# Loading the first 256 rows of x with two neighbouring rows per partition in a SwiGLU kernel

## The chip, the cores and the metric

The kernel runs on one core of a Trainium2 chip. The metric is the device time of one execution in microseconds (us), taken as the median of several runs; lower is better.

## The reference

The reference is a gated feed-forward layer, all tensors bf16:

```python
B, S, D, F = 1, 2048, 640, 1536     # x: (B, S, D)
g = silu(x @ w_gate)                # w_gate: (D, F)
u = x @ w_up                        # w_up:   (D, F)
return (g * u) @ w_down             # w_down: (F, D)
```

## The kernel before

The 2048 rows of x (tokens) are cut into four blocks of 512 (`S_BLK`), and each block into four chunks of 128. D = 640 is five slices of 128 (`KD`, index kd), F = 1536 is twelve (`KF`, index fc or kf).

**A block.** For each fc, `proj` (L197) multiplies the gate weights and the up weights with xT, the transposed x: five matmuls of 512 columns each into the PSUM tiles pg and pu (four buffers in all). `gate` (L212) applies Silu on ScalarE (pg to sg) and multiplies by pu on VectorE into aT. After twelve fc, the down projection follows. Output columns 512 to 639 of all the block's tokens come from twelve matmuls into po_t (L274); ScalarE copies that to ot_t (L283), VectorE transposes it in 32 x 32 squares into ot_q (L285), and ScalarE issues four stores of it (L287), one for each 32 columns, in pieces of 64 bytes. Output columns 0 to 511 come chunk by chunk: twelve matmuls into po_a (L303; the pool tag has two buffers), a copy to ot on ScalarE (L312), a store from SyncE's queue (SP, L321).

**The start.** Tokens 0 to 255 (`PE_X` = 2 chunks) come into x_sb as rows and are transposed on TensorE (`transpose_chunk`, L185: ten transposes into pt, copies to xT by ScalarE for kd 0 and 1 and by VectorE for kd 2 to 4). All other tokens are transposed by the DMA on the way in (`turn_x`, L108). While x is under way, TensorE runs 20 matmuls on ones (`warm`, L175). Then `head` (L221) runs the gate matmuls of fc 0 and 1 for the first 256 tokens: eight of 128 columns for kd 0 and 1 (first chunk 0, then chunk 1), six of 256 columns for kd 2 to 4. Ten up matmuls of 256 columns follow, and then tokens 256 to 511 of the same two fc.

**The first loads.** A DMA is started by the queue of an engine, in the order of that queue. SP starts x chunk 0, the gate weights of fc 0 and 1 for kd 0 and 1 (`K_CUT` = 2), the up weights for kd 2 to 4, and then the transposing load of tokens 256 to 511; ScalarE starts x chunk 1 and the gate weights for kd 2 to 4, and then loads its function table; GpSimd starts the up weights for kd 0 and 1. SP goes on with the rest of the weights, w_down (wd_sb), the next blocks of x and transposed copies of the weights (wgT, wuT).

**Other work.** The last four tokens are computed on VectorE (`row_dots`, L143: 96 multiply-and-sum instructions of x_row with wgT and wuT), spread between VectorE's other work.

**Order.** The head's order on TensorE, ScalarE and GpSimd, and the whole order on VectorE and SP, is kept as written (`keep_order`, L98). From the first block's loop on, the order on TensorE and ScalarE is decided when the program is built: a scheduler goes by its own estimate of when each instruction can run. DMAs started by SP and ScalarE take one of eight completion counters in turn, and a DMA whose counter is still in use waits for the earlier DMA on it.

Of the kernel before, what the change touches and what calls it, by code (L numbers as in the profile page):

```python
# [10 lines left out]
def _body(  # L11
# [8 lines left out]
    nc = tc.nc  # L20
    P = nc.NUM_PARTITIONS
# [8 lines left out]
    x2 = x.rearrange("b s d -> (b s) d")  # L30
    out2 = out.rearrange("b s d -> (b s) d")

    KD = D // P
    KF = F // P
    S_BLK = 512
    NSB = S // S_BLK
    SUB = S_BLK // P
    DA = 512
    Q = 32
# [3 lines left out]
    PE_X = 2  # L43
    K_CUT = 2
# [12 lines left out]
    x_sb = consts.tile([P, PE_X, D], bf16)  # L57
    xT = consts.tile([P, KD, S], bf16)
    wg_sb = consts.tile([P, KD, F], bf16)
    wu_sb = consts.tile([P, KD, F], bf16)  # L60
# [9 lines left out]

    make_identity(nc, ident[:])

    x_v = x2.rearrange("(c p) d -> p c d", p=P)
    xt_v = x2.rearrange("s (kd p) -> s kd p", p=P)
    wg_v = w_gate.rearrange("(kd p) f -> p kd f", p=P)
    wu_v = w_up.rearrange("(kd p) f -> p kd f", p=P)
    wd_v = w_down.rearrange("(kf p) d -> p kf d", p=P)

    def wslice(a, b):
        return slice(a * P, b * P)  # L80

    def load_w(eng, dst, src, a, b):
        eng.dma_start(out=dst[:, :, wslice(a, b)], in_=src[:, :, wslice(a, b)])

    def load_x(eng, c0, c1):
        eng.dma_start(out=x_sb[:, c0:c1, :], in_=x_v[:, c0:c1, :])

    def issue_order(a, b):
        tc.add_manual_dep(
# [18 lines left out]
    def turn_x(c0, c1):  # L108
        s_sl = slice(c0 * P, c1 * P)
        nc.sync.dma_start_transpose(out=xT[:, :, s_sl], in_=xt_v[s_sl])  # L110

    load_x(nc.sync, 0, 1)
    load_x(nc.scalar, 1, 2)
    f_sl = wslice(*W_CHUNKS[0])
    for dst, src, first, second in (
        (wg_sb, wg_v, nc.sync, nc.scalar),
        (wu_sb, wu_v, nc.gpsimd, nc.sync),
    ):
        for eng, k_sl in ((first, slice(0, K_CUT)), (second, slice(K_CUT, KD))):
            eng.dma_start(out=dst[:, k_sl, f_sl], in_=src[:, k_sl, f_sl])  # L120
    turn_x(PE_X, SUB)
    nc.scalar.activation(silu_first[:], ones[:, 0:1], ACT.Silu)
    for a, b in W_CHUNKS[1:]:
# [6 lines left out]
    def turn_w(dst, src):  # L130
# [7 lines left out]
        out=x_row[:],  # L138
        in_=x2[S - T : S, :].rearrange("t d -> (t d)").partition_broadcast(P),
# [29 lines left out]
    def do_dots(n):  # L169
        for _ in range(n):  # L170
            next(dots, None)
# [3 lines left out]
    def warm(n):  # L175
        for _ in range(n):
            nc.tensor.matmul(  # L177
                pw[:, 0:P],
                lhsT=ones[:].broadcast_to([P, P]),
                rhs=ones[:].broadcast_to([P, P]),  # L180
                start=True,
                stop=True,
            )

    def transpose_chunk(c, parts):  # L185
        c_sl = slice(c * P, (c + 1) * P)
        for copy, tag, k0, k1 in parts:
            pt = psum.tile([P, k1 - k0, P], bf16, tag=tag, name="pt")
            for kd in range(k0, k1):
                nc.tensor.transpose(  # L190
                    out=pt[:, kd - k0, :],
                    in_=x_sb[:, c, kd * P : (kd + 1) * P],
                    identity=ident[:],
                )
            copy(out=xT[:, k0:k1, c_sl], in_=pt[:])  # L195

    def proj(ps, w_sb, fc, sb, c0, c1):  # L197
        for kd in range(KD):
            nc.tensor.matmul(  # L199
                ps[:, c0:c1],  # L200
                lhsT=w_sb[:, kd, fc * P : (fc + 1) * P],
                rhs=xT[:, kd, sb * S_BLK + c0 : sb * S_BLK + c1],
                start=(kd == 0),
                stop=(kd == KD - 1),
            )

    def gu_tiles():
        pg = psum.tile([P, S_BLK], f32, tag="gu", name="pg", bufs=4)
        pu = psum.tile([P, S_BLK], f32, tag="gu", name="pu", bufs=4)
        return pg, pu  # L210

    def gate(pg, pu, sb, fc, n_s):  # L212

        s0 = sb * S_BLK
        sg = work.tile([P, S_BLK], f32, name="sg")
        nc.scalar.activation(sg[:, 0:n_s], pg[:, 0:n_s], ACT.Silu)  # L216
        nc.vector.tensor_tensor(  # L217
            out=aT[:, fc, s0 : s0 + n_s], in0=sg[:, 0:n_s], in1=pu[:, 0:n_s], op=ALU.mult
        )

    def head():  # L221

        dve, act = nc.vector.tensor_copy, nc.scalar.copy
        split = [(act, "po_a", 0, 2), (dve, "po_b", 2, KD)]
        late = PE_X * P
        (pg0, pu0), (pg1, pu1) = gu_tiles(), gu_tiles()  # L230
        warm(N_WARM)
        transpose_chunk(0, split)
        transpose_chunk(1, split)
        early = [(kd, c * P, (c + 1) * P) for c in range(PE_X) for kd in range(K_CUT)]
        early += [(kd, 0, late) for kd in range(K_CUT, KD)]
        for kd, c0, c1 in early:
            for fc, pg in ((0, pg0), (1, pg1)):


                nc.tensor.matmul(  # L240
                    pg[:, c0:c1],
                    lhsT=wg_sb[:, kd, wslice(fc, fc + 1)],
                    rhs=xT[:, kd, c0:c1],
                    start=(kd == 0 and c0 == 0),
                    stop=(kd == KD - 1),
                )
        proj(pu0, wu_sb, 0, 0, 0, late)
        proj(pu1, wu_sb, 1, 0, 0, late)
        for fc, pg, pu in ((0, pg0, pu0), (1, pg1, pu1)):
            proj(pg, wg_sb, fc, 0, late, S_BLK)  # L250
            proj(pu, wu_sb, fc, 0, late, S_BLK)
            gate(pg, pu, 0, fc, S_BLK)
        keep_order(mybir.EngineType.PE)
        keep_order(mybir.EngineType.Activation)
        keep_order(mybir.EngineType.Pool)

    head()
    for sb in range(NSB):
        n_s = S_BLK if sb < NSB - 1 else S_BLK - T
        for fc in range(KF):  # L260
            if sb == 0 and fc < 2:
                continue
            pg, pu = gu_tiles()
            proj(pg, wg_sb, fc, sb, 0, n_s)
            proj(pu, wu_sb, fc, sb, 0, n_s)
            gate(pg, pu, sb, fc, n_s)
            if sb > 0 and fc < KF - 2:
                do_dots(2)


        n_t = (SUB if sb < NSB - 1 else SUB - 1) * P
        po_t = psum.tile([P, n_t], f32, tag="po_b", name="po_t")
        for kf in range(KF):
            nc.tensor.matmul(  # L274
                po_t[:],
                lhsT=wd_sb[:, kf, DA:D],
                rhs=aT[:, kf, sb * S_BLK : sb * S_BLK + n_t],
                start=(kf == 0),
                stop=(kf == KF - 1),
            )  # L280
        ot_t = outp.tile([P, n_t], bf16, name="ot_t")
        ot_q = outp.tile([P, n_t], bf16, name="ot_q")
        nc.scalar.copy(ot_t[:], po_t[:])  # L283
        do_dots(3)
        nc.vector.transpose(out=ot_q[:], in_=ot_t[:])  # L285
        for q in range(P // Q):
            nc.scalar.dma_start(  # L287
                out=out2[
                    sb * S_BLK : sb * S_BLK + n_t, DA + q * Q : DA + (q + 1) * Q
                ].rearrange("(i r) c -> r i c", r=Q),  # L290
                in_=ot_q[q * Q : (q + 1) * Q, :].rearrange("r (i c) -> r i c", c=Q),
            )

        for j in range(SUB):
            s0 = sb * S_BLK + j * P
            last = sb == NSB - 1 and j == SUB - 1
            cols = [(0, DA, "po_a")]
            if last:
                cols = [(0, DA // 2, "po_a"), (DA // 2, DA, "po_a"), (DA, D, "po_b")]
            for c0, c1, tag in cols:  # L300
                po = psum.tile([P, c1 - c0], f32, tag=tag, name="po_a")
                for kf in range(KF):
                    nc.tensor.matmul(  # L303
                        po[:],
                        lhsT=aT[:, kf, s0 : s0 + P],
                        rhs=wd_sb[:, kf, c0:c1],
                        start=(kf == 0),
                        stop=(kf == KF - 1),
                    )
                ot = outp.tile([P, c1 - c0], bf16, name="ot" if c1 < D else "ot_b")  # L310
                if c1 < D:
                    nc.scalar.copy(ot[:], po[:])  # L312
                    eng = nc.sync
                else:
                    nc.vector.tensor_copy(out=ot[:], in_=po[:])  # L315
                    eng = nc.sync
                if 0 < j and not last:
                    do_dots(3)
                if sb == NSB - 1 and j == ROW_J:
                    row_tail()  # L320
                eng.dma_start(out=out2[s0 : s0 + P, c0:c1], in_=ot[:])  # L321
        if sb == 0:
            turn_x(2 * SUB, 3 * SUB)
            turn_w(wuT, wut_v)
            turn_x(3 * SUB, 4 * SUB)
# [107 lines left out]
```

## Time and profile before

| what | value |
|---|---|
| median of 3 runs | 163.68 us (163.44 to 163.95) |
| the profiled execution | 163.61 us, of which 162.2 us are the span of its instructions |
| TensorE matmul busy | 159.8 us, 98% of the span |
| VectorE busy | 110.8 us (68%) |
| ScalarE busy | 42.9 us (26%) |
| chain that ended last | TensorE 97%, DMA 2% |
| TensorE from 0 to 2.77 us | 20 warm-up matmuls; x_sb lands at 2.77 |
| TensorE after the last matmul to the end of the span | 1.9 us |

In rows of the profile, PE is TensorE, PEld its weight loads, DVE VectorE, ACT ScalarE, POOL GpSimd, SP SyncE; SPq, ACTq and POOLq are the queues that start DMAs. L190 is line 190 of the kernel. A group's row gives its busy time, the mean duration of one instruction in ns, and the idle time of its engine just before it. A row of the waits reads "who waited <- for whom: us in total, times, longest". A row of the chain or the timeline gives the start in us, the duration, and what ran; a bracket is idle time before it, and what ended that. A row of the DMA issues ends with the time from issue to landing.

### The profile page before, as it was taken

The numbers are of one execution on the slowest core, as the hardware profiler recorded it, in microseconds if no ns is written. First come the engines' busy times: TensorE is split into PE (matmuls) and PEld (weight loads), VectorE is DVE, ScalarE is ACT, GpSimd is POOL, SyncE is SP. The second block draws the span as 40 slices with busy tenths as digits, with TensorE's granted clock in tenths as the row PEclk, the third lists the DMA queues.
The fourth block names the chain that finished last, engine by engine and source line by source line (L and its number), as shares of the span: only waits on it lengthen the run. The fifth ranks groups of instructions, "written<-read, shape, count | busy, mean of one in ns | idle before, by whom it ended". The sixth has DMA issues, their size and how long they took to land.

```text
span 162.2 us, 2119 instructions
## 1 busy us (share of the span) xinstructions
PE 159.8 (98%) x798; PEld 78.1 (48%) x798; DVE 110.8 (68%) x249; ACT 42.9 (26%) x74; POOL 1.5 (1%) x7
## 2 busy tenths in 40 slices
PE   8999999999999999999999999999999999999995
PEld 8854444444444444444444444444444444445454
DVE  1042233599469999979919999979964999993000
ACT  5132222112222222221222322221214222222121
POOL 3000000000000000000000000000000000000000
PEclk9999999999999999999999999999999999999999
DMA  7999999993179996003110000000320000000212
GB/s 215 275 343 350 363 217 220 240 216 87 35 164 161 205 177 136 4 0 34 65 65 0 0 4 2 0 0 1 63 68 33 0 0 0 0 0 4 50 39 73
DMA packets 42217, 15.86 MB, mean 98 GB/s; under 512 B 33216, under 2 KB 42048, under 8 KB 42208
## 3 DMA queue, kind: packets, MB, share of 16 engines
q1 hardware_dynamic: 33680, 14.75, 37.6%
q10 hardware_dynamic: 8480, 0.85, 3.4%
q8 instruction: 6, 0.10, 0.3%
q0 software_dynamic: 48, 0.13, 0.2%
q14 instruction: 3, 0.02, 0.1%
HBM read 6.88 MB, written 2.62 MB: 59 GB/s over the span
## 4 chain that ended last, share of the span: by engine, by line
PE 97%; DMA 2%; DVE 0%; issue 0%
PE pu L199 32%; PE pg L199 31%; PE po_a L303 26%; PE po_t L274 6%; DMA x_sb<-in_x_dram 2%; PE pg L240 1%; PE pt L190 1%; DVE ot_b L315 0%
## 5 line engine op out<-in xcount | busy, mean ns | idle before, releaser
L199 PE MATMUL pu<-xT,wu_sb 128*128 128x512 bf16 (+2 forms) x250 | 59.7, 370 | 0.0
L199 PE MATMUL pg<-xT,wg_sb 128*128 128x512 bf16 (+2 forms) x240 | 58.5, 374 | 0.0
L217 DVE TENSOR_TENSOR aT<-sg,pu 128x512 bf16<-128x512 f32 (+1 forms) x48 | 32.8, 684 | 32.4 <-PE pu L199 28.1
L216 ACT ACTIVATE sg<-pg 128x512 f32<-128x512 f32 (+1 forms) x48 | 28.6, 597 | 70.8 <-PE pg L199 66.2
L303 PE MATMUL po_a<-wd_sb,aT 128*128 128x512 bf16 (+2 forms) x216 | 42.8, 358 | 0.0
L148 DVE SCALAR_TENSOR_TENSOR prod<-wgT,x_row 128x640 f32<-128x640 bf16 x48 | 39.4, 821 | 1.1
L148 DVE SCALAR_TENSOR_TENSOR prod<-wuT,x_row 128x640 f32<-128x640 bf16 x48 | 39.4, 822 | 1.0
L199 PEld LDWEIGHTS <-wu_sb 128*128 128x128 bf16 x250 | 24.5, 98 | 27.3
L199 PEld LDWEIGHTS <-wg_sb 128*128 128x128 bf16 x240 | 23.5, 98 | 26.9
L303 PEld LDWEIGHTS <-aT 128*128 128x128 bf16 x216 | 20.7, 98 | 21.6
L312 ACT CAST ot<-po_a 128x512 bf16<-128x512 f32 (+1 forms) x17 | 9.5, 561 | 32.0 <-PE po_a L303 20.9
L274 PE MATMUL po_t<-aT,wd_sb 128*128 128x512 bf16 (+1 forms) x48 | 10.4, 366 | 0.0
L274 PEld LDWEIGHTS <-wd_sb 128*128 128x128 bf16 x48 | 4.7, 98 | 5.1
L315 DVE CAST ot_b<-po_a 128x128 bf16<-128x128 f32 x1 | 0.3, 292 | 9.9 <-PE po_a L303 9.9
L283 ACT CAST ot_t<-po_t 128x512 bf16<-128x512 f32 (+1 forms) x4 | 2.2, 559 | 11.6 <-PE po_t L274 11.6
L148 DVE DVE_READ_ACCUMULATOR prod<-wuT,x_row 128x1 f32 x48 | 4.0, 83 | 0.0
L148 DVE DVE_READ_ACCUMULATOR prod<-wgT,x_row 128x1 f32 x48 | 3.9, 82 | 0.0
L285 DVE STREAM_TRANSPOSE ot_q<-ot_t 128x512 bf16<-128x512 bf16 (+1 forms) x4 | 2.7, 678 | 1.7 <-ACT ot_t L283 1.7
L195 DVE COPY xT<-pt 128x384 bf16<-128x384 bf16 x2 | 0.7, 358 | 3.5 <-PE pt L190 3.5
L177 PE MATMUL pw<-ones 128*128 128x128 bf16 x20 | 2.3, 310 | 0.3 <-DVE ones L106 0.3
L240 PE MATMUL pg<-xT,wg_sb 128*128 128x128 bf16 (+1 forms) x14 | 2.2, 347 | 0.0
L177 PEld LDWEIGHTS <-ones 128*128 128x128 bf16 x20 | 2.0, 144 | 0.3 <-DVE ones L106 0.3
(16 smaller groups left out, 8.4 us busy)
## 6 DMA issues: line engine op xcount, KB each, us to landing
wd_sb<-in_w_down_dram SPq DMA_DIRECT2D x1, 1920.0 KB, 14.0
out_dram<-ot SPq DMA_DIRECT2D x15, 128.0 KB, 1.7
wg_sb<-in_w_gate_dram SPq DMA_DIRECT2D x2, 640.0 KB, 8.2
wu_sb<-in_w_up_dram SPq DMA_DIRECT2D x2, 640.0 KB, 8.8
x_row<-in_x_dram SPq DMA_DIRECT2D x1, 640.0 KB, 5.2
out_dram<-ot_q ACTq DMA_DIRECT2D x12, 32.0 KB, 1.9
wg_sb<-in_w_gate_dram SPq DMA_DIRECT2D x1, 320.0 KB, 4.4
wu_sb<-in_w_up_dram SPq DMA_DIRECT2D x1, 320.0 KB, 4.9
```

What stands on the lines that cost most here:

```text
L148: nc.vector.scalar_tensor_tensor(out=prod[:], in0=wT[:, fc, :], scalar=1.0, in1=x_row[:, t, :], op0=ALU.mult, op1=ALU.mult, accum_out=acc[ ...
L177: nc.tensor.matmul(pw[:, 0:P], lhsT=ones[:].broadcast_to([P, P]), rhs=ones[:].broadcast_to([P, P]), start=True, stop=True,)
L190: nc.tensor.transpose(out=pt[:, kd - k0, :], in_=x_sb[:, c, kd * P : (kd + 1) * P], identity=ident[:],)
L199: nc.tensor.matmul(ps[:, c0:c1], lhsT=w_sb[:, kd, fc * P : (fc + 1) * P], rhs=xT[:, kd, sb * S_BLK + c0 : sb * S_BLK + c1], start=(kd == 0 ...
L216: nc.scalar.activation(sg[:, 0:n_s], pg[:, 0:n_s], ACT.Silu)
L217: nc.vector.tensor_tensor(out=aT[:, fc, s0 : s0 + n_s], in0=sg[:, 0:n_s], in1=pu[:, 0:n_s], op=ALU.mult)
L240: nc.tensor.matmul(pg[:, c0:c1], lhsT=wg_sb[:, kd, wslice(fc, fc + 1)], rhs=xT[:, kd, c0:c1], start=(kd == 0 and c0 == 0), stop=(kd == KD ...
L274: nc.tensor.matmul(po_t[:], lhsT=wd_sb[:, kf, DA:D], rhs=aT[:, kf, sb * S_BLK : sb * S_BLK + n_t], start=(kf == 0), stop=(kf == KF - 1),)
L283: nc.scalar.copy(ot_t[:], po_t[:])
L285: nc.vector.transpose(out=ot_q[:], in_=ot_t[:])
L303: nc.tensor.matmul(po[:], lhsT=aT[:, kf, s0 : s0 + P], rhs=wd_sb[:, kf, c0:c1], start=(kf == 0), stop=(kf == KF - 1),)
L312: nc.scalar.copy(ot[:], po[:])
```

## The change

The two loads of x rows become one load on SP. Partition p now receives the neighbouring rows 2p and 2p + 1 (2560 bytes in one piece) in place of rows p and 128 + p (two pieces of 1280 bytes). "Chunk" c of the first 256 tokens is then the rows 2p + c. ScalarE's first DMA is the gate weights for kd 0 and 1, its second the up weights for kd 2; SP takes the gate weights for kd 2 to 4 and the up weights for kd 3 and 4. GpSimd's load stays. The stores of these 256 tokens write every second output row: the stores of ot keep their number, and each of the four stores of ot_q in block 0 becomes three (rows 2p, rows 2p + 1, and tokens 256 to 511).

```diff
-    load_x(nc.sync, 0, 1)
-    load_x(nc.scalar, 1, 2)
+    paired = PE_X * P
+
+    def paired_rows(ap):
+        return ap[0:paired, :].rearrange("(p c) d -> p c d", c=PE_X)
+
+    nc.sync.dma_start(out=x_sb[:], in_=paired_rows(x2))
     f_sl = wslice(*W_CHUNKS[0])
-    for dst, src, first, second in (
-        (wg_sb, wg_v, nc.sync, nc.scalar),
-        (wu_sb, wu_v, nc.gpsimd, nc.sync),
+    for eng, dst, src, a, b in (
+        (nc.scalar, wg_sb, wg_v, 0, K_CUT),
+        (nc.sync, wg_sb, wg_v, K_CUT, KD),
+        (nc.gpsimd, wu_sb, wu_v, 0, K_CUT),
+        (nc.scalar, wu_sb, wu_v, K_CUT, K_CUT + 1),
+        (nc.sync, wu_sb, wu_v, K_CUT + 1, KD),
     ):
-        for eng, k_sl in ((first, slice(0, K_CUT)), (second, slice(K_CUT, KD))):
-            eng.dma_start(out=dst[:, k_sl, f_sl], in_=src[:, k_sl, f_sl])
+        eng.dma_start(out=dst[:, a:b, f_sl], in_=src[:, a:b, f_sl])
     turn_x(PE_X, SUB)
...
         nc.vector.transpose(out=ot_q[:], in_=ot_t[:])
+        stores = [(out2[sb * S_BLK : sb * S_BLK + n_t, :], 0, n_t)]
+        if sb == 0:
+            stores = [
+                (paired_rows(out2)[:, c, :], c * P, (c + 1) * P) for c in range(PE_X)
+            ]
+            stores += [(out2[paired:S_BLK, :], paired, S_BLK)]
         for q in range(P // Q):
-            nc.scalar.dma_start(
-                out=out2[
-                    sb * S_BLK : sb * S_BLK + n_t, DA + q * Q : DA + (q + 1) * Q
-                ].rearrange("(i r) c -> r i c", r=Q),
-                in_=ot_q[q * Q : (q + 1) * Q, :].rearrange("r (i c) -> r i c", c=Q),
-            )
+            for rows, t0, t1 in stores:
+                nc.scalar.dma_start(
+                    out=rows[:, DA + q * Q : DA + (q + 1) * Q].rearrange(
+                        "(i r) c -> r i c", r=Q
+                    ),
+                    in_=ot_q[q * Q : (q + 1) * Q, t0:t1].rearrange(
+                        "r (i c) -> r i c", c=Q
+                    ),
+                )
 
         for j in range(SUB):
             s0 = sb * S_BLK + j * P
             last = sb == NSB - 1 and j == SUB - 1
+            rows = out2[s0 : s0 + P, :]
+            if s0 < paired:
+                rows = paired_rows(out2)[:, j, :]
...
-                eng.dma_start(out=out2[s0 : s0 + P, c0:c1], in_=ot[:])
+                eng.dma_start(out=rows[:, c0:c1], in_=ot[:])
```

More of the change, by code (lines that the diff above doesn't have):

```diff
@@ L71, in _body @@
     make_identity(nc, ident[:])
-    x_v = x2.rearrange("(c p) d -> p c d", p=P)
     xt_v = x2.rearrange("s (kd p) -> s kd p", p=P)
@@ L83, in load_w @@
         eng.dma_start(out=dst[:, :, wslice(a, b)], in_=src[:, :, wslice(a, b)])
-    def load_x(eng, c0, c1):
-        eng.dma_start(out=x_sb[:, c0:c1, :], in_=x_v[:, c0:c1, :])
     def issue_order(a, b):
@@ L228, in head @@
         split = [(act, "po_a", 0, 2), (dve, "po_b", 2, KD)]
-        late = PE_X * P
         (pg0, pu0), (pg1, pu1) = gu_tiles(), gu_tiles()
@@ L234, in head @@
         early = [(kd, c * P, (c + 1) * P) for c in range(PE_X) for kd in range(K_CUT)]
-        early += [(kd, 0, late) for kd in range(K_CUT, KD)]
+        early += [(kd, 0, paired) for kd in range(K_CUT, KD)]
         for kd, c0, c1 in early:
@@ L246, in head @@
                 )
-        proj(pu0, wu_sb, 0, 0, 0, late)
-        proj(pu1, wu_sb, 1, 0, 0, late)
+        proj(pu0, wu_sb, 0, 0, 0, paired)
+        proj(pu1, wu_sb, 1, 0, 0, paired)
         for fc, pg, pu in ((0, pg0, pu0), (1, pg1, pu1)):
-            proj(pg, wg_sb, fc, 0, late, S_BLK)
-            proj(pu, wu_sb, fc, 0, late, S_BLK)
+            proj(pg, wg_sb, fc, 0, paired, S_BLK)
+            proj(pu, wu_sb, fc, 0, paired, S_BLK)
             gate(pg, pu, 0, fc, S_BLK)
```

## The prediction

> **What bounds the kernel now.** I read the page's chain first, then the waits, the chain in order of time, the timeline of the first 7 us and of 28 to 47 us, and the table of DMA issues.
>
> ```profile
> PE 97%; DMA 2%; DVE 0%; issue 0%
> L199 PE MATMUL pu<-xT,wu_sb 128*128 128x512 bf16 (+2 forms) x250 | 59.7, 370 | 0.0
> PEld L190 <- DMA x_sb<-in_x_dram: 0.5, 1, 0.5
> 0.00 2.77 DMA x_sb<-in_x_dram
> 2.81 1.25 PE pt L190 x10
> 4.06 1.99 PE pg L240 x14
> 6.05 1.09 PE pu L199 x10
> ```
>
> The chain is one stretch of TensorE work: it waits for x until 2.77 us and never again; the large groups have 0.0 us of idle time before them. So only the first microseconds can give anything, and anything that makes TensorE wait later is a loss. The last two lines hold a second fact. The 14 gate matmuls are 8 x 128 + 6 x 256 = 2560 columns and take 1.99 us; the 10 up matmuls are also 2560 columns and take 1.09 us. TensorE runs at half pitch (0.107 us for 128 columns, starts of single matmuls in the trace) until 5.78 us, where the trace's first clock record also begins (PEclk prints 1.00 before it too, for want of a record), and at full pitch from there. A delay before 5.78 us therefore costs half of itself, if the step up stays where it is.
>
> ```profile
> 0.30 2.05 PEld L177 LDWEIGHTS <-ones 128*128 128x128 bf16 x20 [0.30 <-DVE ones L106]
> 2.81 0.99 PEld L190 LDWEIGHTS <-x_sb 128*128 128x128 bf16 x10 [0.46 <-DMA x_sb<-in_x_dram]
> 3.75 1.97 PEld L240 LDWEIGHTS <-wg_sb 128*128 128x128 bf16 x14
> 5.78 1.08 PEld L199 LDWEIGHTS <-wu_sb 128*128 128x128 bf16 x10
> ```
>
> Warm-up matmuls fill 0.30 to about 2.41 us (the 20th starts at 2.31), x opens the transposes at 2.81, and gate and up weights follow with no bracket: they had landed. The bracket at 2.81 is the only wait at the start.
>
> ```profile
> wg_sb<-in_w_gate_dram ACTq DMA_DIRECT2D x1, 192.0 KB, 3.7
> x_sb<-in_x_dram SPq DMA_DIRECT2D x1, 160.0 KB, 2.8
> x_sb<-in_x_dram ACTq DMA_DIRECT2D x1, 160.0 KB, 3.0
> wg_sb<-in_w_gate_dram SPq DMA_DIRECT2D x1, 128.0 KB, 3.2
> wu_sb<-in_w_up_dram POOLq DMA_DIRECT2D x1, 128.0 KB, 4.2
> ```
>
> **Part 1, x as one load.** Before, chunk 0 lands at 2.77 and chunk 1, issued at 0.13, at 3.17 (trace), in time for its first transpose at 3.32. After, chunk 0 must wait for all 320 KB. In the packet records the two loads lie one behind the other: the first runs from 1.02 to 2.40, the second from 1.75 to 2.81 us, 55 ns for each 1280 bytes, and the last share is 0.3 us behind the others both times. One load of 128 pieces of 2560 bytes carries the same bytes in the same order. No row shows that size. If it takes 2 x 55 ns, x lands where chunk 1 landed, 3.17; going by the fastest tenth of the 5120-byte packets (196 ns), 2560 bytes take some 102 ns and it lands about 3.10. Bounds: 2.77 (the doubled bytes cost nothing) and 3.6 (the 0.43 us that each engine needs for its 16 gate packets of 27 ns, now first on ScalarE's queue, get in between). I take 3.15, nearest to the chunk 1 row, so TensorE starts its transposes 0.38 us later, at 3.19. At half pitch that is 0.19 us of work at the end; both ends give 0 to +0.4.
>
> The Trainium skill (DMA: Bandwidth & Descriptors, Anatomy of one DMA) fits a GpSimd load as 2.0 us plus bytes over 436 GB/s. An estimate by that would land 320 KB at 2.75 us and make this term nothing; chunk 1's landing speaks against it.
>
> **Part 2, gate pieces 0 and 1 first on ScalarE's queue.** They landed at 3.63 and the first gate weight load starts at 3.75, held by TensorE's own order, so getting them sooner is worth nothing: no wait for wg_sb stands in the list. After, they lie behind the same x bytes, about 3.6 again, and are needed at 4.1. Pieces 2 to 4 (4.27 before) move to SP behind x and are needed at 5.0; up piece 2 moves to ScalarE, up 0 and 1 stay on GpSimd (5.27, needed near 6.0). The bytes ahead of each piece are nearly unchanged and every need moves later: 0. Without that cover, each 0.1 us late would cost 0.05 to 0.1.
>
> Issue times: SP still issues three loads ahead of the transposing load (0.39, 0.42 and 0.47 us; now a 128-, a 384- and a 256-piece one), so the queue behind keeps its times. ScalarE issues two, as before, ahead of its table load. 0.
>
> **Part 3, stores of block 0.** Out rows keep their number and size of pieces; what grows is ScalarE's issues, 4 to 12.
>
> ```profile
> 30.75 2.75 PE L274 MATMUL po_t<-aT,wd_sb 128*128 128x512 bf16 x12
> 33.34 10.52 PE L303 MATMUL po_a<-wd_sb,aT 128*128 128x512 bf16 x48
> 34.90 1.98 ACTq L287 DMA_DIRECT2D out_dram<-ot_q  x4
> 36.92 0.59 ACT L312 CAST ot<-po_a 128x512 bf16<-128x512 f32 x1 [2.80 <-DMA out_dram<-ot_q]
> ```
>
> ScalarE takes its queue in order: behind the stores stand the copies that free the two po_a buffers, then the first Silu of block 1. One store issue took 322 to 501 ns with 512 pieces; the new ones have 128 (eight) and 256 (four), and loads of 128 and 256 pieces took 0.39 and 0.42. With 0.04 us between: 8 x 0.40 + 4 x 0.46 = 5.0 us, so 34.9 to 39.9, and the first copy ends at 40.5. In the old order TensorE would want that buffer at 38.68 (33.50 + 24 x 0.216) and stall near 2 us. But the changed program's instruction order moves work: after 24 po_a matmuls come 12 gate and up matmuls of block 1 (2.6 us), then the other 24. The buffer is then wanted at 41.27, 0.75 us after the copy: 0. Bounds: at 0.32 an issue, 39.2; at 0.50, 41.4 and a copy done at 42.0, a stall of 0.7 us. I take the cover as holding, nearest to the 128-piece rows.
>
> Every DMA of SP and ScalarE takes one of eight counters in turn and waits for that counter's last user. Stores 6 to 8 wait for the wgT loads, the last issued at 31.8 and landed by 36.7, and store 8 comes up near 37.8; store 9 waits for store 1, 34.9 + 1.9. Eight more DMAs are one full turn, so later pairings stay. SP's stores of rows 2 and 3 go out 2.6 us later, and behind them the transposing loads for block 2 (landing near 51 at present, used at 82.7), wuT (used from 90.0) and block 3: hidden by tens of microseconds. VectorE's order is unchanged.
>
> **Sum.** 163.61 (profiled execution: span 162.2 and 1.4 around it) + 0.19 + 0 + 0 = 163.80; the median of the runs shown lies 0.07 above that execution: 163.9 us. About 0.3%, 0.49 us, is what a measurement here can tell from no change: faster is below 163.2, slower above 164.2.
>
> **Rivals.**
> x lands no later (2.77): 163.7. The even run of 55 ns packets, 16 engines at once, speaks against it.
>
> The step to full pitch follows the start of the transposes. It came 2.97 us after 2.81; 2.97 after 3.19 is 6.16, and the whole 0.38 is lost: 164.1.
>
> Slower: the step up is missed. The pause ahead of the transposes doubles from 0.40 (2.41 to 2.81) to 0.78 us. If the step needs an almost unbroken run, and the pause breaks it, TensorE starts over: the first run-up took 5.48 us (0.30 to 5.78), from 3.19 that is 8.67, so 2.89 us more at half pitch, +1.45, with the 0.19 some 165.3. For it: 2.1 us of warm-up alone did not bring the step. Against it: a pause of 0.40 did not prevent it. It decides from a pause somewhere between 0.40 and 0.78 or not at all. The Trainium skill (TensorE: Matmul & The Clock Gate, What's actually happening) has a free-running window of about 3.4 us that must be busy; an estimate by it puts the next chance at 9.2 us and the time at 165.6. No run here shows a second chance.
>
> Slower: ScalarE's issues cost 0.50 each, the cover in part 3 is gone, 0.19 + 0.7: 164.6. The existing 64-byte stores speak for it (three of four took 0.50), their four times larger piece count against.
>
> Faster: the step up isn't tied to this kernel's work and falls over 1.4 us sooner, -0.7 + 0.19: 163.2 or less. The four executions known lie within 0.51 us, about 1 us of that step, which speaks against it.
>
> **Numbers.** Forecast 0.28; x no later 0.08; step follows 0.14; step missed 0.25; issues uncovered 0.15; step sooner 0.10. Of the forecast 0.05, and of the step that follows 0.08, spill over 164.2 by the scatter of a quarter microsecond. Slower: 0.25 + 0.15 + 0.05 + 0.08 = 0.53; faster 0.10; within 0.3% 0.37. Cases of both signs do not hold most of the chance, but two sizes do; the forecast's own range is 163.5 to 164.2. The range for 8 in 10 leaves out most of the faster case and the far end of the missed step: 163.3 to 165.6.
>
> **What would show it.** x_sb landing 3.1 to 3.2 us from issue and the first transpose near 3.19; the 14 gate matmuls starting near 4.24, and full pitch from near 5.8; no gap ahead of any wg_sb or wu_sb weight load; twelve ScalarE issues in about 5 us; no idle time ahead of po_a. A po_a wait for ScalarE, half pitch past 6.5 us, or a first transpose before 2.9 would prove the forecast wrong.

## The result, and the profile after

The changed kernel takes 165.18 us (median of 6 runs, 165.11 to 165.56), the kernel before beside it 163.58 us (6 runs, 162.98 to 163.95): a ratio of 1.0103, 95% interval 1.0081 to 1.0125. It is slower by about 1.6 us. The profiled execution took 165.11 us with a span of 163.7 us, 1.5 us more than before.

The page of the changed kernel, part 4 (shares of the chain that ended last) and one group of part 5 (busy us, mean ns | idle us just before, releaser):

```profile
PE 73%; SPq 14%; DMA 6%; ACTq 3%; DVE 2%; issue 1%; ACT 0%; DVEq 0%
L316 PE MATMUL po_a<-wd_sb,aT 128*128 128x512 bf16 (+2 forms) x216 | 43.0, 358 | 1.9 <-ACT ot L325 1.9
```

Before, the chain was 97% TensorE. Now a quarter of it runs elsewhere: through SP's loads, a landing, VectorE and ScalarE's queue. TensorE has one long wait, and it is for ScalarE's copies out of po_a. The timeline around it (start, duration, what ran, idle time before):

```profile
32.78 5.34 PE L316 MATMUL po_a<-wd_sb,aT 128*128 128x512 bf16 x24
35.07 6.87 ACTq L295 DMA_DIRECT2D out_dram<-ot_q  x12
41.98 1.07 ACT L325 CAST ot<-po_a 128x512 bf16<-128x512 f32 x2 [8.40 <-DMA out_dram<-ot_q]
42.61 5.34 PE L316 MATMUL po_a<-wd_sb,aT 128*128 128x512 bf16 x24 [1.90 <-ACT ot L325]
```

The twelve store issues hold ScalarE for 6.87 us; both copies stand behind them, and TensorE goes on at 42.61, as soon as the first copy is done. Single issues, in the chain in order of time:

```profile
36.43 0.46 ACTq L295
...
36.93 1.58 ACTq L295
...
38.55 0.44 ACTq L295
```

Eleven issues took 0.35 to 0.46 us, the fifth 1.58. The start of the same execution:

```profile
3.00 0.98 PE L192 MATMUL pt<-ident,x_sb 128*128 128x128 bf16 x10 [0.38 <-DMA x_sb<-in_x_dram]
3.86 1.46 PE L241 MATMUL pg<-xT,wg_sb 128*128 128x128 bf16 x14
5.15 1.26 PE L201 MATMUL pu<-xT,wu_sb 128*128 128x256 bf16 x10
```

x opens the transposes at 3.00 (2.81 before), but the gate matmuls take 1.46 us instead of 2.20: full pitch came near 3.6 us here and at 5.78 before, so the first up matmul starts at 5.15 instead of 5.89.

That gives the whole difference. In every profiled execution, the start of the last matmul is the start of the first up matmul, plus the wait in block 0, plus 154.16 to 154.18 us, plus whatever else delays TensorE right after the first up matmul. Before: 5.89 + 0 + 154.16 = 160.05. After: 5.15 + 2.06 (between matmul starts, from 40.55 to 42.61) + 154.16 + 0.18 = 161.55. The 0.18 us stand ahead of the gate matmuls of tokens 256 to 511, which start at 6.43; the transposing load of these tokens lands at 6.39.

### The profile page after: what moved, and what is told of

Read it like the earlier page. It is cut to its first block, busy times and chain, and to the rows that moved or that the text cites. A ratio compares the mean times of both kernels' runs of the same rounds, so it can differ in the third digit from the quotient of the medians.

```text
span 163.7 us, 2130 instructions
## 1 busy us (share of the span) xinstructions
PE 159.1 (97%) x798; PEld 77.2 (47%) x798; DVE 110.8 (68%) x249; ACT 42.7 (26%) x74; POOL 1.5 (1%) x7
## 4 chain that ended last, share of the span: by engine, by line
PE 73%; SPq 14%; DMA 6%; ACTq 3%; DVE 2%; issue 1%; ACT 0%; DVEq 0%
PE pu L201 23%; PE pg L201 23%; PE po_a L316 23%; SPq L106 8%; DMA wgT<-in_w_gate_dram 5%; PE po_t L275 4%; SPq L82 3%; ACTq L295 3%; DVE prod L150 2%; SPq L128 1%; DMA out_dram<-ot_q 1%; SPq L122 1%; DVE ot_q L286 0%; ACT ot L325 0%; SPq L139 0%
```

## The experiments

Theory A: ScalarE's store issues in block 0 hold back the copies that free po_a. Rival B: the later x costs the time. Rival C: TensorE's changed order around block 0 costs it. Theory Q and rival P came after the first four runs and ask what made one issue long: Q the transposing loads of wgT ahead of the stores, P a packet of 16,384 bytes that the trace shows on a queue of kind "instruction". All ratios are to the kernel before, run beside.

**The changed start alone.**

```diff
-        if sb == 0:
+        if False:
             stores = [
```

> The changed start (one load of x, ScalarE's gate pieces first) with the four block-0 stores of columns 512 to 639 as before; the row order of those columns of the first 256 rows is left out. Theory A (the twelve store issues on ScalarE hold back the copies that free po_a): the stall of about 2 us in block 0 is gone, 163.5 to 163.9 us, same as before within 0.3%, first transpose near 3.0 us. Rival B (the later x costs the time): 165.2 us. Rival C (TensorE's changed order around block 0 costs the time): the old order comes back with the four stores, so 163.5 to 163.9 as well.

Measured: 163.74 us, ratio 1.0021 (1.0004 to 1.0038). The four stores and the old order are back, and so is the old timing:

```profile
3.10 1.25 PE L192 MATMUL pt<-ident,x_sb 128*128 128x128 bf16 x10 [0.47 <-DMA x_sb<-in_x_dram]
34.94 1.98 ACTq L295 DMA_DIRECT2D out_dram<-ot_q  x4
36.96 0.59 ACT L325 CAST ot<-po_a 128x512 bf16<-128x512 f32 x1 [2.80 <-DMA out_dram<-ot_q]
```

No wait in block 0. B falls as the main cause: the start is worth 0.1 to 0.6 us of the 1.6.

**The stores alone.**

```diff
+        parts = [(0, P), (P, 2 * P), (2 * P, n_t)] if sb == 0 else [(0, n_t)]
         for q in range(P // Q):
-            nc.scalar.dma_start(
+            for t0, t1 in parts:
+                nc.scalar.dma_start(
...
```

> The start and the row order as before; each of the four block-0 stores of columns 512 to 639 cut into three (tokens 0 to 127, 128 to 255, 256 to 511). Theory A: twelve issues take about 6.9 us, TensorE waits 1.5 to 2 us for a po_a buffer, 165.0 to 165.4 us. Rival B: 163.6 us. Rival C: the changed order is there, 165.2 us.

Measured: 164.71 us, ratio 1.0091 (1.0061 to 1.0122). That is less than was expected, but twelve issues on the old start, without paired rows, bring some 1.3 of the 1.6 us:

```profile
35.35 7.20 ACTq L289 DMA_DIRECT2D out_dram<-ot_q  x12
42.59 1.07 ACT L316 CAST ot<-po_a 128x512 bf16<-128x512 f32 x2 [8.27 <-DMA out_dram<-ot_q]
43.23 4.48 PE L307 MATMUL po_a<-wd_sb,aT 128*128 128x512 bf16 x20 [1.76 <-ACT ot L316]
```

**The stores on SP.**

```diff
-                nc.scalar.dma_start(
+                (nc.sync if sb == 0 else nc.scalar).dma_start(
                     out=rows[:, DA + q * Q : DA + (q + 1) * Q].rearrange(
```

> The changed kernel with the twelve block-0 stores started by SP instead of ScalarE. Theory A: ScalarE's copy of the first po_a follows at once, no wait ahead of po_a, 163.5 to 163.9 us; the twelve issues sit on SP for 5 to 7 us and delay its own stores without harm. Rival B: 165.2 us. Rival C: the old order comes back, 163.5 to 163.9 us. If the bytes of the stores rather than their issues cost the time: 165.2 us.

Measured: 163.97 us, ratio 1.0044 (1.0025 to 1.0063). The bytes and the issues are those of the changed kernel; only the engine that issues them is another. The issues last as long, and nobody waits:

```profile
34.97 6.89 SPq L295 DMA_DIRECT2D out_dram<-ot_q  x12
35.73 0.58 ACT L325 CAST ot<-po_a 128x512 bf16<-128x512 f32 x1 [2.00 <-PE po_a L316]
```

The copy is done at 36.3, and TensorE's matmuls of block 0 run without a gap. A stands. Of the 0.6 us that are left, 0.4 lie outside the span of the kernel's instructions: time less span is 1.81 to 1.86 us in all six executions, against 1.36 to 1.45 in those of the kernel before. The span alone is 0.15 us longer than before (medians, 162.15 against 162.0). Why the time outside the span grows, no run shows.

**TensorE in the written order.**

```diff
+    keep_order(mybir.EngineType.PE)
     keep_order(mybir.EngineType.DVE)
```

> The changed kernel with TensorE held to the written order: all 48 po_a matmuls of block 0 ahead of block 1. Theory A: TensorE needs the first po_a buffer 2.6 us sooner and ScalarE frees it no sooner, so the wait grows from 2.1 to about 4.6 us and the time to 167.4 to 168 us. Rival C: the old order is the cure, 163.6 us. Rival B: 165.2 us.

Measured: 167.03 us, ratio 1.0223 (1.0179 to 1.0267).

```profile
41.15 1.07 ACT L325 CAST ot<-po_a 128x512 bf16<-128x512 f32 x2 [6.54 <-DMA out_dram<-ot_q]
41.79 5.34 PE L316 MATMUL po_a<-wd_sb,aT 128*128 128x512 bf16 x24 [2.62 <-ACT ot L325]
```

C falls: the scheduler's order is a cover, not a cost. Without its twelve gate and up matmuls the kernel loses near 2 us more. The wait in this execution is 2.8 us between starts, not 4.6, for two reasons: no issue was long here (the twelve took 5.72 us for 6.87), and full pitch came late, so the first up matmul started at 6.24 instead of 5.15 and TensorE wanted the buffer later. So the long issue comes and goes.

**What makes one issue long.** First without transposing loads in front of the stores.

```diff
-    turn_w(wgT, wgt_v)
+    for a in range(0, KF, WT_STEP):
+        nc.sync.dma_start(
+            out=wgT[:, a : a + WT_STEP, :], in_=wd_v[:, a : a + WT_STEP, :]
+        )
```

> The changed kernel with the three transposing loads of wgT replaced by plain loads of w_down rows of the same size, so the values that go into the last four tokens are other ones. In the changed kernel's profile one of the twelve issues took 1.58 us, the others 0.44 to 0.46. Theory Q (the wgT transposing packets in front of the stores hold it up, and their landing at 31.7 us sets when the stores begin): the stores begin near 34.4, no issue over 0.6 us, the twelve end near 40.3, 163.8 to 164.3 us. Rival P (a 16,384-byte packet of the instruction queue, seen at 37.1 us, holds one DMA engine): one issue of about 1.5 us remains, 164.4 to 165.2 us.

Measured: 165.25 us, ratio 1.0105 (1.0076 to 1.0134). wgT had landed by 34.05 us, and still:

```profile
37.30 0.44 ACTq L298
37.78 1.36 ACTq L298
39.19 0.46 ACTq L298
```

Q falls as the reason for the long issue. (The stores also did not begin sooner, at 35.44: TensorE was slower to full pitch in this execution, and the copy of po_t came later.)

Then with the packet moved.

```diff
-    N_WARM = 20
+    N_WARM = 40
...
-                pw[:, 0:P],
-                lhsT=ones[:].broadcast_to([P, P]),
-                rhs=ones[:].broadcast_to([P, P]),
+                pw[0:64, 0:64],
+                lhsT=ones[:].broadcast_to([P, 64]),
+                rhs=ones[:].broadcast_to([P, 64]),
```

> The changed kernel with 40 warm-up matmuls of 64 x 64 in place of 20 of 128 x 128: 40 more TensorE instructions, so what TensorE fetches by count of instructions comes some 20 matmuls, about 4 us, sooner. Rival P: the 16,384-byte packet moves from about 37.1 to about 33 us, no issue over 0.6 us, the twelve issues take 5.8 us, 164.0 to 164.5 us. Theory Q: the long issue stays, 165.0 to 165.4 us.

Measured: 164.19 us, ratio 1.0055 (1.0035 to 1.0074). In the packet records the 16,384-byte packet is now at 32.82 us.

```profile
34.48 5.80 ACTq L295 DMA_DIRECT2D out_dram<-ot_q  x12
40.95 5.34 PE L316 MATMUL po_a<-wd_sb,aT 128*128 128x512 bf16 x23 [0.20 <-ACT ot L325]
L295 ACTq DMA_DIRECT2D out_dram<-ot_q x24: 322/462/516, 34.5 to 151.6; - x24
```

The last line is the source view (min/median/max ns of an issue): the longest is 516, where the changed kernel has 1578. Not all of the shorter wait (0.37 us between starts for 2.06) is the packet's: 1.07 us come from the issues (5.80 us for 6.87) and 0.59 from an earlier begin (34.48 for 35.07), which follows wgT's landing in this execution (31.15 for 31.74). This execution was also the fastest of its ten. By the ratios the gain is some 0.8 us, near the 1.1 us of a long issue; the executions without a trace may have begun their stores later (on ScalarE the begin lies between 34.48 and 35.44 us over all profiles).

P holds in every profile with many block-0 issues. With the packet among them an issue took 0.99 us or more: packet at 37.14 (1.58 us, changed kernel), 37.42 (1.65, stores alone), 37.32 (1.53, on SP's queue), 37.73 (1.36, plain wgT), 36.97 (0.99, early transpose below). In all five the long issue ends 0.34 to 0.42 us after the packet does. With the packet elsewhere none took over 0.70 us: 42.86 (written order), 32.82 (here), 42.20 (eight stores below), 32.82 and 33.39 (the two runs at the end). These packets belong to the queue of kind "instruction" (part 3 of the page: 6 packets, 0.10 MB) and last 0.9 to 1.8 us each. The second of the six begins when 406 to 438 TensorE instructions (matmuls and weight loads) have started, in every profile, and 40 more such instructions moved it by over 4 us: it follows TensorE's instruction count. How the packet holds up the issue is not shown by itself. That one DMA engine delays its share of the stores, and that the queue then has no room for the next, is argued from the landings (stores 2 to 5 of the changed kernel land together, from 39.16 to 39.65).

The control, the small warm-up in the kernel before:

> The kernel before with 40 warm-up matmuls of 64 x 64 in place of 20 of 128 x 128, the control for the run with the shifted packet. The 16,384-byte packet near 38.6 us lies behind the four stores there and should move near 33 to 34 us: 163.2 to 163.6 us, no change. If the small warm-up itself makes a kernel faster (an earlier full pitch): 162.5 to 163.0 us.

Measured: 163.62 us, ratio 1.0011 (0.9997 to 1.0024). The packet moved to 33.86 and nothing was gained: the small warm-up by itself is not what made the run above faster.

**Eight issues.**

```diff
+                nc.scalar.dma_start(
+                    out=out2[0:paired, cols].rearrange(
+                        "(i r c) d -> r c i d", c=PE_X, r=Q
+                    ),
...
```

> The changed kernel with the two paired stores of each 32 columns joined into one of four dimensions: 8 issues in block 0 instead of 12. Theory A: at 0.49 us each they end near 39 us, the first copy at 39.6; the scheduler now puts only three gate matmuls (0.65 us) ahead of the second half of po_a, which wants its buffer near 38.8 to 39.3: a wait of 0.3 to 0.8 us, 163.9 to 164.5 us, between 4 and 12 issues. If the start or the bytes set the time: 165.2 us.

Measured: ratio 1.0137 (1.0086 to 1.0189), about 165.6 us: above the expectation and no better than twelve.

```profile
37.66 0.60 ACTq L292 DMA_DIRECT2D out_dram<-ot_q  x1
38.30 0.61 ACTq L300 DMA_DIRECT2D out_dram<-ot_q  x1
...
40.23 1.07 ACT L328 CAST ot<-po_a 128x512 bf16<-128x512 f32 x2 [6.02 <-DMA out_dram<-ot_q]
40.87 5.34 PE L319 MATMUL po_a<-wd_sb,aT 128*128 128x512 bf16 x23 [1.45 <-ACT ot L328]
```

The mechanism held, the size did not: each issue took 0.60 us instead of 0.45, those with three dimensions (L300) too, so the eight last 5.20 us, only 0.5 us less than twelve without a long one (5.72), while the scheduler put 3 instead of 12 matmuls in between, 1.9 us less cover.

**An earlier transpose of ot_q.**

```diff
-        do_dots(3)
+        if sb > 0:
+            do_dots(3)
         nc.vector.transpose(out=ot_q[:], in_=ot_t[:])
+        if sb == 0:
+            do_dots(3)
```

> The changed kernel with VectorE's three row products of block 0 moved from ahead of the ot_q transpose to behind it. Theory A: the stores begin 0.7 to 0.8 us sooner (near 34.3), everything behind them on ScalarE too, and TensorE's wait shrinks by as much: 164.3 to 164.6 us. If the stores' end is set by the DMA engines (wgT in front of them) and not by their begin: unchanged, 165.2 us.

Measured: 164.98 us, ratio 1.0108 (1.0078 to 1.0138). In the profiled execution (163.96 us, the fastest of its runs) the stores begin at 34.51 and TensorE waits 0.73 us; the median shows no gain. Inconclusive: the other executions have no trace.

**The x load alone.** The first gate and up loads go back to their old queues.

> The kernel before with x as one load alone: the first gate and up loads on the queues that they had, four block-0 stores, the row order of columns 512 to 639 of the first 256 rows left out. In the start-only run x landed near 3.05 us and the time was 0.34 us (0.04% to 0.38%) over the kernel before. If the later x is all of that: 163.6 to 163.9 us here too. Gate pieces 0 and 1 now stand behind x and ScalarE's 192 KB and should land near 4.2, wanted near 4.1 us: a wait of 0.1 to 0.2 us at half pitch, up to 0.1 us more. If the moved gate and up loads were the cost: 163.4 us.

Measured: 163.38 us, ratio 1.0003 (0.9985 to 1.0021). x landed at 2.93, the weight load of the gate pieces waited 0.2 us, and the time did not move beyond its interval. It is the time that was expected if the moved gate and up loads were the cost. But the intervals of this and of the whole start overlap, so how the start's 0 to 0.6 us divides stays open.

**Two cures at once.** Shifted packet with early transpose, then shifted packet with stores on SP.

> The changed kernel with both: the shifted packet (40 small warm-up matmuls) and the three row products of block 0 behind the ot_q transpose. Theory A: the twelve issues take 5.8 us from near 34, the first copy is done near 40.4, before TensorE wants the buffer at 40.7 to 41.3, no wait, and the time falls to that of the changed start alone: 163.5 to 164.0 us. If something else in the block-0 stores costs time: 164.2 us and more.

Measured: 164.50 us, ratio 1.0063 (1.0041 to 1.0085): not the time of the start alone, and no better than the shifted packet by itself. The wait is 0.26 us in the profile, whose execution took 163.86 us; what the slower ones lost, no trace shows.

```profile
34.88 5.79 ACTq L298 DMA_DIRECT2D out_dram<-ot_q  x12
40.71 1.07 ACT L328 CAST ot<-po_a 128x512 bf16<-128x512 f32 x2 [6.61 <-DMA out_dram<-ot_q]
```

> The changed kernel with both: the shifted packet (40 small warm-up matmuls) and the twelve block-0 stores started by SP. ScalarE is then not held at all and no issue should be long. Theory A: only the changed start is left, 163.4 to 163.8 us, the level of the start-only run (1.0021) or below. If some part of the excess has nothing to do with ScalarE or the long issue (the stores' own traffic, the rows written in pairs): 164.0 us as with the stores on SP alone.

Measured: 164.19 us, ratio 1.0051 (1.0033 to 1.0070). No wait in block 0, no issue over 0.50 us. Yet it lies above what was expected, and above the start alone (1.0021) and the small warm-up (1.0011) together. The excess lies outside the span of the instructions: here too, as with the stores on SP alone, time less span is 1.74 to 1.86 us in every execution, where every execution of the other kernels has 1.35 to 1.47. By the medians of the spans it is 0.45 us longer than the kernel before (162.4 against 161.95), no more than the start (162.3 against 162.0) and the small warm-up (162.2 against 161.95) together. So starting the twelve stores on SP costs some 0.4 us that no instruction in the span shows; its cause stays open. The profiled execution has one more wait, at the start:

```profile
PEld L201 <- DMA wg_sb<-in_w_gate_dram: 0.4, 1, 0.4
8.97 0.39 PE L201 MATMUL pg<-xT,wg_sb 128*128 128x512 bf16 x1 [0.17 <-DMA wg_sb<-in_w_gate_dram]
```

Full pitch came near 3.9 us here, and TensorE wanted the next gate weights 0.33 us (between starts) before they landed at 8.93. What an early full pitch gives can thus be lost again to a load. No version with paired rows beat the kernel before.

## Why the prediction was right and wrong

The time lies in the range, slower was the likeliest sign, and the rival that came true was named with its place (ScalarE's issues uncovered). But it had a chance of 0.15, the forecast of 163.9 took the cover as holding, and even the rival's price was too low: 0.7 us against 2.06. That 165.18 lies inside the range is luck: the upper end of 165.6 and the largest chance of a slower time (0.25) came from the missed step to full pitch, which did not happen, and the rival that did happen would have given 164.6 by its price.

**Part 3 failed, in four terms.** (1) The issue time: I took 0.36 us for 128 pieces (the row of the load says 0.39) and 0.42 for 256, from loads, 5.0 us in all; in a row an issue starts every 0.48 to 0.49 us, and twelve last 5.7. The 0.50 us of the existing stores, kept as a bound, was the better row. (2) The long issue, 1.1 us more, for which I had no term. (3) The begin, 35.07 for 34.90: it came from VectorE, whose products waited for wgT's landing at 31.74 (31.14 before). These make the copy ready at 42.57 instead of 40.5. (4) The buffer was wanted sooner, at 40.55 instead of 41.27: by 0.56 us because TensorE had come to full pitch sooner (0.74, less the 0.18 at 6.14), and by 0.16 because I counted from the chain's 33.50, where the first po_a matmul starts at 33.34. The slack of 0.75 and these terms: 0.17 + 0.74 + 1.12 + 0.72 - 0.75 = 2.0, the wait in the trace. I also treated the cover as there or gone; its 2.6 us was there all along (the written order costs near 2 us more), only not long enough.

**Part 1 held for the landing.** 2560 bytes took 102 ns a packet, as worked out from the 5120-byte ones; x landed at 2.84 to 3.16 over the profiles with one load, the forecast being 3.15. The landing before was that of one execution: with the old loads chunk 0 landed at 2.77, 2.37 and 2.31 us in three profiles. The start cost 0.34 us (0.1 to 0.6) against 0.19, which neither shows nor refutes that the delay costs half of itself; and full pitch did not stay at 5.78. The Trainium skill's fit for GpSimd loads gives an estimate of 2.75 us (DMA: Bandwidth & Descriptors, Anatomy of one DMA), below every landing of the one load.

**Part 2 held** in the changed kernel's profile: no wait for gate or up weights ahead of the first up matmul. The loads behind them had less slack than I thought once full pitch came early: 0.18 us lost at 6.14 here, 0.33 at 8.5 in the last run.

**The rivals on the clock.** Full pitch began anywhere from 3.6 to 6.6 us in the profiles, at 3.6 (changed kernel) after a pause of 0.6 us and at 6.5 (written order) after one of 0.65. So the missed step, at 8.67, did not happen, and the pause does not decide. The step that follows the transposes is refuted: it came 0.6 us after the first transpose in the changed kernel and 3.4 us after it in the written order, with the same start. The step that isn't tied to the kernel's work is what the profiles look like. The spread, 3 us, would fit the window of some 3.4 us that runs freely (the Trainium skill, TensorE: Matmul & The Clock Gate, What's actually happening); no run here shows the window itself, and the 500 ns either way that the section gives for the variation are exceeded.

**Faster** needed a sooner step. The profiled execution had one, worth 0.74 us at the first up matmul, and the wait in block 0 took it back: ScalarE's end was not moved by it.

## What to carry to other kernels

Count a DMA's issue on a compute engine as work of that engine, at the rate of issues in a row, and look what is queued behind it: splitting four stores into twelve moved no more bytes and cost 1% through two copies. Put many small issues on a queue that has nothing urgent behind them; here SP did the same twelve for less than half the loss. And a cover that a scheduler makes is as long as its own estimate of the delay, so compare its length with the longest delay that the rows allow, not with the likeliest.

## What the runs showed of the hardware

Issues in a row with 128 or 256 pieces of 64 bytes take 0.44 to 0.46 us each on ScalarE and 0.43 to 0.45 on SP, starting every 0.48 to 0.49 us; the first one takes 0.35 on ScalarE and 0.50 on SP. Where every second store had a fourth dimension in its pattern, all took 0.60. The Trainium skill (DMA: Bandwidth & Descriptors, Issuing engines are not separate DMA queues) calls the issue time "usually small relative to the DMA itself". For one store that holds here, 0.45 us against 1.5 to 3.7 to its landing; but twelve of them, 5.7 us, hold the engine longer than any landing takes.

Packets of 16,384 bytes, six per execution and about 1 us each, come over a queue of kind "instruction", each at nearly the same count of TensorE's instructions in every profile (406 to 438 for the second). Where one met a row of small stores, one issue took 1.0 to 1.65 us and ended about 0.4 us after the packet; in the profile with 40 more instructions it met none, and no issue was long.

The same twelve stores started by SP instead of ScalarE added 0.4 us to the time outside the span of instructions, in all 18 executions.

The start of full pitch varied by 3 us, from 3.6 to 6.6, between executions with the same start. Whoever compares two profiles should read the first full-pitch matmul before anything else.
